# Masked words and conversion words in PSUM banks, casts of P on ScalarE alone, in a fused sparse-attention and feed-forward kernel

## The chip, the cores and the metric

The kernel runs on one core of one Trainium2 chip. A core has five engines, each with an instruction stream of its own that runs in order: TensorE (PE, matrix products; its weight loads are shown as PEld), VectorE (DVE), ScalarE (ACT), GpSimd (POOL) and SyncE (SP), which here only issues transfers. SBUF is the working memory of 128 partitions. PSUM is the memory that PE writes, in eight banks of 512 words a partition; DVE and ACT read and write it too, POOL doesn't. The metric is the device time of one execution in microseconds (us), the median of several runs.

## What is computed

Block-sparse attention over 4 × 8 heads of 768 positions with 64 dimensions, and behind it a feed-forward part in which g = h − tanh(h):

```python
scores = scale * np.matmul(q, k.transpose(0, 1, 3, 2))
...
scores = np.where(mask, scores, -1000000000.0)
scores = scores - np.max(scores, axis=-1, keepdims=True)
attn = np.exp(scores)
attn = attn / (np.sum(attn, axis=-1, keepdims=True) + 1e-09)
return np.matmul(attn, v).astype(np.float32)
...
h = x @ w_in
g = h - np.tanh(h)
return (g @ w_out).astype(np.float32)
```

`mask` lets a block of 32 positions see its neighbours, the first and the last block, and three drawn blocks. x is the attention's output, 3072 tokens of 512; w_in is 512 × 2048, w_out 2048 × 512. The inputs are 32-bit floats, but the weights arrive as 64-bit words that the kernel turns into 32-bit ones ("converts").

## The kernel before

**Precision by parts.** PE multiplies with fewer bits than the inputs have. So operands are split into a high and a low part, and products of parts are summed. For q and k, `mask_words` (line 183) clears the low 12 bits of each word (`bitwise_and` with −4096) and `low_words` (line 191) subtracts the result from the word: what is left is the low part `lo`, which lies in the same tile where the masked word lay. Each pair of heads has q and k side by side in one tile `rawx` of 1536 columns, handled as two halves of 768: both masks and the first subtraction run on DVE, the second subtraction on POOL. The tiles `lo` and `rawx` each have two buffers.

**The pieces of attention.** The heads go in 16 pairs (`pr`), and each pair has six steps `n` (96 in all). In a step PE makes three banks of trial scores for a row maximum (`smax`), which DVE reduces (`most`, tile `mc`), and three banks of final scores (`scores`), which ACT turns into exponentials (`exps`, tile `pe`). The exponentials P are split as well: `high` (line 292) casts them to 16 bits, tile `ph`, in two ACT operations of 768 columns, except for one step in six, `n % 6 in PH_DVE`, where DVE casts 1536 columns at once; `low` (line 301) takes the rest on POOL, tile `pl`. `accum` multiplies both with V (tile `vhl`), `norm` divides. The maxima of a head go back into the operands by a small transfer (`most_send`, tile `nm`). `pe` has three buffers, `ph` and `pl` four.

**Banks.** Two PSUM banks hold the products with V. The six others form a ring: whoever calls `bank()` gets the next one, and so must wait until the user of six calls before has been read out:

```python
        turn = iter(range(10**6))
        ps = lambda: banks[next(turn) % 6], banks[6:]
```

**The order.** Nothing is left to a scheduler here. `at(time, f, ...)` (line 342) collects pieces of work with due times; a step n has the length 2, a pair 12. The list is sorted by time (line 435) and carried out in that order, and each engine keeps to the order in which its instructions were written (class `InOrder`). SP's transfers go through one queue in the same order: the loads of `rawx`, the twelve transfers a pair that spread it and `lo` over the operand tiles `slot` (`dist`), `nm`, and the results.

**Conversions.** Six weight tiles are converted during attention: `load_pre` fetches 64-bit words, `convert_pre` (line 403) makes 32-bit ones by three DVE operations (`convert_op`, line 449), at due times 2 apart, and sends them out to memory. They recur every 24, so in every other pair. The feed-forward part converts the other tiles by the same three operations (`convert`, line 465), there with a PSUM bank for the words in between. That part (`FFN`) has an order of its own; the diff doesn't touch it.

Of the kernel before, what the change touches and what calls it, by code (L numbers as in the profile page):

```python
# [15 lines left out]
I32 = mybir.dt.int32  # L16
AF = mybir.ActivationFunctionType
ALU = mybir.AluOpType
# [24 lines left out]
W0, DW = 42.9, 24  # L43
# [7 lines left out]

LEAD = 12
LAV = 5.35
PH_DVE = (3,)
RAMP, NRAMP = 4, 24
LATE = {2: (14, 10, 6), 3: (8, 4, 3), 4: (5, 3, 2), 5: (2, 1, 1), 6: (1, 0.5, 0.5)}

# [32 lines left out]
@with_exitstack  # L90
def attention_ffn(ctx, tc, kq, v, samp, w_in, w_out, blocks, out):
    nc = tc.nc
    cst = ctx.enter_context(tc.tile_pool(name="cst", bufs=1))
    dpool = ctx.enter_context(tc.tile_pool(name="dpool", bufs=1, space=DRAM))
    xscr = [dpool.tile([P, T, DM], F32, name=f"xscr{b}") for b in range(B)]

    ident = cst.tile([P, P], F32, name="ident")
    make_identity(nc, ident)
    bias = [cst.tile([P, 1], F32, name=f"bias{i}") for i in range(2)]
    for x, val in zip(bias, (QB, THR2)):  # L100
        nc.vector.memset(x, val)

    slots = [cst.tile([P, 4, 2, S], F32R, name=f"slot{i}") for i in range(NSLOT)]
    wt = {(m, ft): dpool.tile([P, 512], F32, name=f"w{m}{ft}") for ft in range(NPRE) for m in "io"}
    part = [dpool.tile([P, DM], F32, name=f"part{j}") for j in range(CT)]
    f2 = ctx.enter_context(tc.tile_pool(name="f2", bufs=2))
    stage = [cst.tile([P, 1024], I32, name=f"stage{i}") for i in range(2)]
    ffn = FFN(tc, w_in, w_out, xscr, ident, bias, slots, wt, out, f2, part, stage)
    with ExitStack() as actx:
        psum = actx.enter_context(tc.tile_pool(name="psum", bufs=1, space=PSUM))  # L110
        banks = [psum.tile([P, 512], F32, name=f"ps{i}") for i in range(8)]
        turn = iter(range(10**6))
        ps = lambda: banks[next(turn) % 6], banks[6:]
        ffn.one = lambda name: ps[0]()
        ffn.nc = InOrder(tc)
        attention(actx, tc, kq, v, samp, w_in, w_out, blocks, xscr, ident, ps, slots, wt, f2, ffn)
        ffn.nc = tc.nc
    with ExitStack() as fctx:
        ffn.rest(fctx)


def attention(ctx, tc, kq, v, samp, w_in, w_out, blocks, xscr, ident, ps, slots, wt, f2, ffn):
    nc = InOrder(tc)
    bank, av = ps
# [5 lines left out]
    raws, rvs, los, ams, sbs = {}, {}, {}, {}, {}  # L130
# [49 lines left out]
    def half(pr, x):  # L180
        return slice(x * S, (x + 1) * S)

    def mask_words(pr, x):
        if x == 0:
            los[pr] = p2.tile([P, 2 * S], F32, tag="lo", name=f"lo{pr}", bufs=2)
        c = half(pr, x)
        nc.vector.tensor_scalar(
            out=los[pr].bitcast(I32)[:, c], in0=raws[pr].bitcast(I32)[:, c], scalar1=-4096, scalar2=None, op0=ALU.bitwise_and
        )

    def low_words(pr, x, eng):
        c = half(pr, x)
        eng.tensor_tensor(out=los[pr][:, c], in0=raws[pr][:, c], in1=los[pr][:, c], op=ALU.subtract)

    def dist(pr, j, what):
        i = pr % NSLOT
# [95 lines left out]
    def high(n, e):  # L292
        if e == 0:
            phs[n] = p2.tile([P, 2 * S], F16, tag="ph", name=f"ph{n}", bufs=PB)
        if n % 6 not in PH_DVE:
            c = half(None, e)
# [45 lines left out]
    def at(time, f, *args):  # L342
        ev.append((time, len(ev), f, args))
# [12 lines left out]
    for pr in range(NPAIR):  # L356
        t0 = 12 * pr
        late = LATE.get(pr, (0, 0, 0))
        at(t0 - 36 + late[0] if pr > 1 else -18.5 if pr else -49, load_x, pr)
        at(t0 - 15.5 if pr > 1 else 1 if pr else -18, load_v, pr)  # L360
        s = t0 + late[1]
        when = (s - 29.2, s - 25.2, s - 23.2) if pr > 1 else (-1, 0.7, 2.8) if pr else (-28, -28, -28)
        at(when[0], mask_words, pr, 0)
        at(when[1], mask_words, pr, 1)
        at(when[2], low_words, pr, 0, nc.vector)
        at(when[2], low_words, pr, 1, nc.gpsimd)
        for x, (j, what) in enumerate(ORDER):
            at(t0 + late[2] - 21 + x if pr > 1 else x - 3 if pr else EARLY[x], dist, pr, j, what)
        s = t0 + (10.5, 4)[pr] if pr < 2 else t0
        at(s - 9.3, v_most, pr)  # L370
        at(s - 7.54, v_turn, pr)
        at(s - 7.28, v_scale, pr)
        at(t0 + (8.45, 4, 0)[min(pr, 2)] - 4.45, v_parts, pr, 0)
        at(t0 + (7, 4, 0)[min(pr, 2)] - 2.3, v_parts, pr, 1)
        at(t0 + 16.4, spill, pr)
# [21 lines left out]
    wraw = {}  # L397
# [5 lines left out]
    def convert_pre(m, ft, k):  # L403
        if k == 0:
            wcv[m, ft] = f2.tile([P, 512], I32, tag="wcvt", name=f"cvt{m}{ft}")
        convert_op(nc, wraw[m, ft], wcv[m, ft], wcv[m, ft], k)
        if k == 2:
            nc.sync.dma_start(out=wt[m, ft], in_=wcv.pop((m, ft)).bitcast(F32))

    wcv = {}  # L410
    for x in range(2 * NPRE):
        at(W0 + DW * x, load_pre, "io"[x % 2], x // 2)
        for k in range(3):
            at(W0 + DW * x + 6 + 2 * k, convert_pre, "io"[x % 2], x // 2, k)
    xa = x_parts(slots[(NPAIR - 3) % NSLOT].rearrange("p a j s -> p (a j s)"))
    xn = {}

# [31 lines left out]
def convert_op(nc, raw, t, tmp, k):  # L449
    w = raw.rearrange("p (n w) -> p n w", w=2)  # L450
    if k == 0:
        nc.vector.tensor_scalar(
            out=tmp, in0=w[:, :, 1], scalar1=3, scalar2=0x3FFFFFF8, op0=ALU.logical_shift_left, op1=ALU.bitwise_and
        )
    elif k == 1:
        nc.vector.scalar_tensor_tensor(
            out=tmp, in0=w[:, :, 1], scalar=-0x40000000, in1=tmp, op0=ALU.bitwise_and, op1=ALU.bitwise_or
        )
    else:
        nc.vector.scalar_tensor_tensor(  # L460
            out=t, in0=w[:, :, 0], scalar=29, in1=tmp, op0=ALU.logical_shift_right, op1=ALU.bitwise_or
        )
# [18 lines left out]
def x_parts(area):  # L481
    n = NCT * P * CT
    return [area[:, i * n : (i + 1) * n].rearrange("p (c n) -> p c n", c=NCT) for i in range(2)]
# [224 lines left out]
```

## Time and profile before

| | us |
|---|---|
| three runs: median (lowest to highest) | 1006.49 (1005.1 to 1008.77) |
| the profiled execution | 1005.82 |
| its span, first to last instruction | 1004.0 |
| busy in the span: PE | 914.0 |
| DVE | 786.9 |
| ACT | 625.9 |
| POOL | 519.4 |

The busy times are of the whole span and mix its two halves, attention up to about 460 us and the feed-forward part behind it. In the rows below, an arrow reads "output from inputs" (`lo<-rawx` writes `lo` and reads `rawx`; a `pf` or `ps` is a PSUM bank), the shape is partitions × elements, `x3` counts merged instructions, and a bracket gives the idle time before an instruction and what ended it. L79 is the line of the helper through which all attention work is recorded, so there the tiles tell the operations apart.

### The profile page before, as it was taken

The numbers are of one execution on the slowest core, as the hardware profiler recorded it, in microseconds if no ns is written. First come the engines' busy times: TensorE is split into PE (matmuls) and PEld (weight loads), VectorE is DVE, ScalarE is ACT, GpSimd is POOL, SyncE is SP. The second block draws the span as 40 slices with busy tenths as digits, with TensorE's granted clock in tenths as the row PEclk, the third lists the DMA queues.
The fourth block names the chain that finished last, engine by engine and source line by source line (L and its number), as shares of the span: only waits on it lengthen the run. The fifth ranks groups of instructions, "written<-read, shape, count | busy, mean of one in ns | idle before, by whom it ended". The sixth has DMA issues, their size and how long they took to land.

```text
span 1004.0 us, 18122 instructions
## 1 busy us (share of the span) xinstructions
PE 914.0 (91%) x7072; PEld 752.5 (75%) x7072; DVE 786.9 (78%) x1222; ACT 625.9 (62%) x1013; POOL 519.4 (52%) x247
## 2 busy tenths in 40 slices
PE   2887889998988888977999999999999999999997
PEld 1676777776777776866778888888888888888885
DVE  5797999999999998837999976666676666667664
ACT  0576767777777776874666665554555565555553
POOL 2586987888788888792455532222222222222221
PEclk9898989899999999978999999999999999999999
DMA  8746676767676757334362210120020001001001
GB/s 218 190 113 150 166 194 162 179 169 179 169 179 163 187 138 164 112 105 138 113 191 79 85 64 22 37 79 22 1 74 1 1 1 43 1 0 43 1 1 42
DMA packets 54100, 99.74 MB, mean 99 GB/s; under 512 B 5768, under 2 KB 26440, under 8 KB 54016
## 3 DMA queue, kind: packets, MB, share of 16 engines
q1 hardware_dynamic: 53704, 97.81, 36.4%
q8 instruction: 55, 0.90, 0.4%
q10 hardware_dynamic: 312, 0.79, 0.3%
q14 instruction: 29, 0.24, 0.1%
HBM read 44.64 MB, written 15.20 MB: 60 GB/s over the span
## 4 chain that ended last, share of the span: by engine, by line
PE 62%; DVE 24%; DMA 7%; issue 4%; ACT 2%; SPq 0%; POOL 0%; DVEq 0%; ACTq 0%; POOLq 0%
PE pf L561 25%; PE ps L79 12%; DVE mc L79 9%; PE pf L593 8%; PE pf L594 8%; PE pf L595 8%; DVE lo L79 5%; DVE vhl L79 2%; DMA slot<-nm 2%; DMA slot<-lo 2%; DVE ph L79 1%; DMA xscr<-xq 1%; DVE xq L79 1%; PE pf L475 1%; DVE cvto L79 1%
## 5 line engine op out<-in xcount | busy, mean ns | idle before, releaser
L79 POOL TENSOR_TENSOR pl<-pe,ph 128x1536 f16<-128x1536 f32 x96 | 313.6, 3281 | 87.0 <-ACT ph L79 41.8
L79 PE MATMUL ps<-slot 89*128 89x512 f32 (+5 forms) x1152 | 271.1, 376 | 55.5 <-DVE mc L79 31.1
L584 POOL TENSOR_TENSOR gl<-t,gh 128x512 fp32r<-128x512 f32 x94 | 121.5, 1293 | 336.3 <-ACT gh L583 292.2
L79 PEld LDWEIGHTS ps<-slot 89*128 89x128 f32 (+2 forms) x1152 | 189.8, 205 | 89.8 <-DVE mc L79 44.6
L79 ACT ACTIVATE pe<-ps 128x512 f32<-128x512 f32 x288 | 169.1, 592 | 102.4 <-PE ps L79 94.2
L79 DVE TENSOR_REDUCE mc<-ps 128x1 f32<-128x512 f32 (+1 forms) x288 | 186.6, 679 | 25.8 <-PE ps L79 25.5
L576 DVE TENSOR_TENSOR t<-t,pf 128x512 f32<-128x512 f32 x94 | 64.5, 686 | 122.8 <-ACT t L570 122.7
L79 PEld LDWEIGHTS <-ph 128*128 128x128 f16 x2304 | 117.7, 101 | 27.5 <-issue 27.2
L79 ACT ACTIVATE ph<-pe 128x768 f16<-128x768 f32 x160 | 135.0, 844 | 5.0
L79 PE MATMUL ps<-vhl,ph 128*128 128x65 f16 (+1 forms) x2304 | 129.7, 200 | 3.2 <-DVE vhl L79 2.3
L583 ACT ACTIVATE gh<-t 128x512 fp32r<-128x512 f32 x94 | 59.4, 632 | 116.1 <-DVE t L580 114.1
L79 PE MATMUL ps<-vhl,pl 128*128 128x65 f16 x1152 | 124.4, 198 | 6.2 <-POOL pl L79 6.2
L79 PEld LDWEIGHTS <-pl 128*128 128x128 f16 x1152 | 111.8, 103 | 9.0 <-POOL pl L79 9.0
L568 ACT ACTIVATE u<-pf 128x512 f32<-128x512 f32 x94 | 56.2, 598 | 78.4 <-PE pf L561 78.0
L580 DVE COPY_PREDICATED t<-mk,pf 128x512 f32<-128x512 int32 x94 | 69.7, 742 | 6.9 <-DVE pf L579 0.5
L593 PE MATMUL pf<-wx,gh 128*128 128x512 f32 x192 | 74.7, 389 | 0.0
L594 PE MATMUL pf<-wx,gh 128*128 128x512 f32 x192 | 74.7, 389 | 0.0
L579 DVE SCALAR_TENSOR_TENSOR pf<-qq,pf 128x512 f32<-128x512 f32 x94 | 65.3, 694 | 7.5
L561 PE MATMUL pf<-slot,wx 128*128 128x512 f32 x288 | 70.3, 391 | 0.4 <-DVE t L580 0.4
L561 PE MATMUL pf<-xbuf,wx 128*128 128x512 f32 x288 | 69.5, 390 | 0.0
L572 ACT ACTIVATE qq<-u,bias 128x512 f32<-128x512 f32 x94 | 68.3, 727 | 0.0
L574 ACT ACTIVATE mk<-u,bias 128x512 f32<-128x512 f32 x94 | 67.8, 721 | 0.0
(113 smaller groups left out, 1564.2 us busy)
## 6 DMA issues: line engine op xcount, KB each, us to landing
slot<-rawx SPq DMA_DIRECT2D x128, 192.0 KB
slot<-lo SPq DMA_DIRECT2D x64, 192.0 KB
rawx<-kq SPq DMA_DIRECT2D x15, 768.0 KB
stage<-w_in SPq DMA_DIRECT2D x13, 512.0 KB
stage<-w_out SPq DMA_DIRECT2D x13, 512.0 KB
rawv<-v SPq DMA_DIRECT2D x16, 384.0 KB
xscr<-xq SPq DMA_DIRECT2D x16, 384.0 KB
out<-ob SPq DMA_DIRECT2D x24, 256.0 KB
```

Source lines behind the costliest of these rows:

```text
L79: r = f(*args, **kw)
L561: nc.tensor.matmul(h, lhsT=w[:, cc], rhs=x[:, c, :], start=(k == 0), stop=(k == 3 * NCT - 1))
L572: nc.scalar.activation(out=qq, in_=u, func=AF.Square, scale=QS, bias=qbias)
L574: nc.scalar.activation(out=mk, in_=u, func=AF.Relu, scale=-1.0, bias=tbias)
L576: nc.vector.tensor_tensor(out=t, in0=t, in1=h, op=ALU.subtract)
L579: nc.vector.scalar_tensor_tensor(out=h, in0=qq, scalar=QC, in1=h, op0=ALU.add, op1=ALU.mult)
L580: nc.vector.copy_predicated(t, mk.bitcast(I32), h)
L583: nc.scalar.activation(out=gh, in_=t, func=AF.Copy)
L584: nc.gpsimd.tensor_tensor(out=gl, in0=t, in1=gh.bitcast(F32), op=ALU.subtract)
L593: nc.tensor.matmul(o, lhsT=gh[:, c], rhs=wo[0][ft], start=(ft == f0), stop=False)
L594: nc.tensor.matmul(o, lhsT=gh[:, c], rhs=wo[1][ft], start=False, stop=False)
L595: nc.tensor.matmul(o, lhsT=gl[:, c], rhs=wo[0][ft], start=False, stop=(ft == f1 - 1))
```

## The change

- The masked words no longer lie in `lo`: each mask writes a bank of the ring, and the subtraction reads that bank and writes `lo`. The 1536 columns of a pair go in three pieces of 512 (a bank's size) in place of two halves. A piece's subtraction follows its mask at once, all on DVE; the three pieces are due at s − 29.2, s − 27.2 and s − 23.2. POOL's subtraction is gone.
- `PH_DVE` is empty: all casts to `ph` are ACT's, two in each step.
- In the six conversions of attention the words in between go to a bank of the ring; the three operations are due 0.45 apart in place of 2.

```diff
-PH_DVE = (3,)
+PH_DVE = ()
...
+    his = {}
+
     def mask_words(pr, x):
         if x == 0:
             los[pr] = p2.tile([P, 2 * S], F32, tag="lo", name=f"lo{pr}", bufs=2)
-        c = half(pr, x)
+        b = his[pr, x] = bank()
         nc.vector.tensor_scalar(
-            out=los[pr].bitcast(I32)[:, c], in0=raws[pr].bitcast(I32)[:, c], scalar1=-4096, scalar2=None, op0=ALU.bitwise_and
-        )
-
-    def low_words(pr, x, eng):
-        c = half(pr, x)
-        eng.tensor_tensor(out=los[pr][:, c], in0=raws[pr][:, c], in1=los[pr][:, c], op=ALU.subtract)
+            out=b.bitcast(I32), in0=raws[pr].bitcast(I32)[:, 512 * x : 512 * (x + 1)], scalar1=-4096, scalar2=None, op0=ALU.bitwise_and
+        )
+
+    def low_words(pr, x):
+        c = slice(512 * x, 512 * (x + 1))
+        nc.vector.tensor_tensor(out=los[pr][:, c], in0=raws[pr][:, c], in1=his.pop((pr, x)), op=ALU.subtract)
...
-        when = (s - 29.2, s - 25.2, s - 23.2) if pr > 1 else (-1, 0.7, 2.8) if pr else (-28, -28, -28)
-        at(when[0], mask_words, pr, 0)
-        at(when[1], mask_words, pr, 1)
-        at(when[2], low_words, pr, 0, nc.vector)
-        at(when[2], low_words, pr, 1, nc.gpsimd)
+        when = (s - 29.2, s - 27.2, s - 23.2) if pr > 1 else (-1, 0.7, 2.8) if pr else (-28, -28, -28)
+        for x in range(3):
+            at(when[x], mask_words, pr, x)
+            at(when[x], low_words, pr, x)
...
-        convert_op(nc, wraw[m, ft], wcv[m, ft], wcv[m, ft], k)
+            wcp[0] = bank().bitcast(I32)
+        convert_op(nc, wraw[m, ft], wcv[m, ft], wcp[0], k)
...
-            at(W0 + DW * x + 6 + 2 * k, convert_pre, "io"[x % 2], x // 2, k)
+            at(W0 + DW * x + 6.05 + 0.45 * k, convert_pre, "io"[x % 2], x // 2, k)
```

DVE's order around the first mask of pair 9 (`lo9` from `rawx9`; `ps` is a bank of the ring, `nm` the maxima sent), before:

```order
L79 TENSOR_SCALAR lo9_2882<-rawx9_2655 128x768
L79 TENSOR_REDUCE mc15_2878<-ps1_95 128x2
L79 TENSOR_REDUCE mc15_2878<-ps3_97 128x1
L79 CAST ph39_2888<-pe39_2872 128x1536
L79 TENSOR_REDUCE mc15_2878<-ps5_99 128x1
L79 TENSOR_SCALAR nm14_2949<-ps1_95 6x128
L79 TENSOR_REDUCE mc15_2878<-ps2_96 128x2
```

and now:

```order
L79 TENSOR_SCALAR ps1_95<-rawx9_2679 128x512
L79 TENSOR_TENSOR lo9_2906<-rawx9_2679,ps1_95 128x512
L79 TENSOR_REDUCE mc15_2902<-ps0_94 128x2
L79 TENSOR_REDUCE mc15_2902<-ps3_97 128x1
L79 TENSOR_REDUCE mc15_2902<-ps5_99 128x1
L79 TENSOR_SCALAR nm14_2975<-ps1_95 6x128
L79 TENSOR_SCALAR ps3_97<-rawx9_2679 128x512
L79 TENSOR_TENSOR lo9_2906<-rawx9_2679,ps3_97 128x512
L79 TENSOR_REDUCE mc15_2902<-ps2_96 128x2
```

The mask of 768 columns became mask and subtraction of 512, the cast is gone, and a second piece stands where only maxima stood. The third piece stands where the second mask and DVE's subtraction were, about one step apart.

ACT's order in step 63, the fourth of pair 10 (`pe63`), with the scaling of V (`vhl`) and the next step behind it, before:

```order
L79 ACTIVATE pe63_4538<-ps4_98 128x512
L79 ACTIVATE pe63_4538<-ps0_94 128x512
L79 ACTIVATE pe63_4538<-ps2_96 128x512
L79 ACTIVATE vhl2_110<-rawv11_4191,sb11_4477 128x12x64
L79 ACTIVATE pe64_4603<-ps4_98 128x512
```

and now:

```order
L79 ACTIVATE pe63_4574<-ps5_99 128x512
L79 ACTIVATE pe63_4574<-ps1_95 128x512
L79 ACTIVATE ph63_4591<-pe63_4574 128x768
L79 ACTIVATE pe63_4574<-ps4_98 128x512
L79 ACTIVATE vhl2_110<-rawv11_4226,sb11_4515 128x12x64
L79 ACTIVATE ph63_4591<-pe63_4574 128x768
L79 ACTIVATE pe64_4641<-ps0_94 128x512
```

The two casts of 768 columns came into this step, as they stand in the other five of the pair.

More of the change, by code (lines that the diff above doesn't have):

```diff
@@ L405, in convert_pre @@
             wcv[m, ft] = f2.tile([P, 512], I32, tag="wcvt", name=f"cvt{m}{ft}")
-        convert_op(nc, wraw[m, ft], wcv[m, ft], wcv[m, ft], k)
+            wcp[0] = bank().bitcast(I32)
+        convert_op(nc, wraw[m, ft], wcv[m, ft], wcp[0], k)
         if k == 2:
             nc.sync.dma_start(out=wt[m, ft], in_=wcv.pop((m, ft)).bitcast(F32))
-    wcv = {}
+    wcv, wcp = {}, [None]
     for x in range(2 * NPRE):
```

## The prediction

> **What bounds the kernel now.** I read the page's slices first, then the busy times by stage, then one period of VectorE (DVE) in order of time. The run has two halves. Attention ends near 460 us; then the feed-forward half runs with TensorE (PE) full.
>
> ```profile
> PE   2887889998988888977999999999999999999997
> DVE  5797999999999998837999976666676666667664
> PE 62%; DVE 24%; DMA 7%; issue 4%; ACT 2%; SPq 0%; POOL 0%; DVEq 0%; ACTq 0%; POOLq 0%
> ```
>
> The slices are 25.1 us each. In attention PE has eights and DVE nines; behind slice 20 PE has nines to the end. So what the change saves before 460 us moves the start of a PE-bound half by as much; nothing in the diff touches that half's own work.
>
> Attention treats one pair of heads after another, and each pair has one DVE CAST (of `ph`, n%6 = 3). The time between two CASTs is a period:
>
> ```profile
> 184.01:210.58 26.57, 24.30 (x293) 20.06 (x292) 26.29 (x41) 19.08 (x29) 22.32 (x7) 0.87 0.64 164
> 263.45:288.05 24.60, 21.78 (x293) 17.67 (x292) 24.15 (x38) 19.86 (x30) 22.04 (x7) 1.00 0.66 164
> 288.05:314.44 26.39, 23.53 (x293) 19.18 (x292) 26.11 (x42) 19.50 (x29) 22.28 (x7) 0.94 0.66 170
> 365.40:387.29 21.89, 19.60 (x273) 15.97 (x273) 21.38 (x38) 17.91 (x27) 20.87 (x7) 1.00 0.52 129
> ```
>
> The columns are length, busy PE, PE loads, DVE, ACT, POOL, then the granted clock. The plain period takes 24.60 us, and DVE is busy for 24.15 of it; no other engine passes 22.1. A period with three conversion operations (288.05) takes 1.79 more, and DVE's busy time grows by 1.96. A period with a mask fewer (365.40) takes 2.71 less, and DVE's falls by 2.77. The period follows DVE nearly one to one: **DVE is the bound of attention.**
>
> What DVE does there, in order of time (start, length):
>
> ```profile
> 263.45 0.94 DVE L79 CAST ph<-pe 128x1536 f16<-128x1536 f32 x1
> 264.32 0.68 DVE L79 TENSOR_REDUCE mc<-ps 128x1 f32<-128x512 f32 x1
> ...
> 269.82 1.99 DVE L79 TENSOR_SCALAR lo<-rawx 128x768 int32<-128x768 int32 x1
> 271.73 1.28 DVE L79 TENSOR_REDUCE mc<-ps 128x2 f32<-128x512 f32 x2
> ...
> 273.72 1.88 DVE L79 TENSOR_TENSOR lo<-rawx,lo 128x768 f32<-128x768 f32 x1
> 275.52 1.87 DVE L79 TENSOR_REDUCE mc<-ps 128x2 f32<-128x512 f32 x3
> ...
> 283.91 3.03 DVE L79 TENSOR_SCALAR lo<-rawx 128x768 int32<-128x768 int32 x1
> 286.85 1.28 DVE L79 TENSOR_REDUCE mc<-ps 128x2 f32<-128x512 f32 x2
> ```
>
> The same mask at the start of the run, with GpSimd (POOL) not yet at work, and the subtraction there:
>
> ```profile
> 8.03 0.95 DVE L79 TENSOR_TENSOR lo<-rawx,lo 128x768 f32<-128x768 f32 x1
> 18.73 0.55 DVE L79 TENSOR_SCALAR lo<-rawx 128x768 int32<-128x768 int32 x1
> ```
>
> So 0.55 us of mask becomes 1.99 and 3.03 beside POOL, whose `pl` operations last over 3 us each. Most of that time DVE stands and waits for POOL.
>
> **Part 1: masks into PSUM, low parts from there.** From start to next start the plain period loses 1.91 (269.82), 1.80 (273.72) and 2.94 (283.91): 6.65 us. It gains three pairs of a mask of 512 words into a bank and a subtraction that reads that bank. Attention shows no such operation; the feed-forward half shows its like: SBUF words into PSUM, then SBUF with PSUM.
>
> ```profile
> L452 DVE TENSOR_SCALAR pf<-stage x26: 678/691/720, 464.1 to 575.8; 128x512 int32<-128x512 int32 x26
> 464.06 0.69 DVE L452 TENSOR_SCALAR pf<-stage 128x512 int32<-128x512 int32 x1
> 464.79 0.69 DVE L456 SCALAR_TENSOR_TENSOR pf<-stage,pf 128x512 int32<-128x512 int32 x1
> 472.60 0.69 DVE L460 SCALAR_TENSOR_TENSOR cvti<-stage,pf 128x512 int32<-128x512 int32 x1
> 473.21 0.68 DVE L576 TENSOR_TENSOR t<-t,pf 128x512 f32<-128x512 f32 x1
> 500.00:550.00 50.00, 49.76 (x218) 40.55 (x218) 48.22 (x80) 32.92 (x58) 25.70 (x20) 1.00 0.45 137
> ```
>
> POOL is busy for half of that stretch (25.70 of 50.00), yet none of 26 took over 720 ns: the wait on POOL is gone in this form. A step with a dependent successor costs 0.73, one with an independent successor 0.61. A pair costs 1.34, three cost 4.0. Bounds: 0.55 and 0.95 (free, above) at the low end, 4.5 for three; today's waits stay at the high end, 3 × (1.91 + 1.80) = 11.1. I take 4.0, the row's. DVE: −2.65 per period.
>
> Left alone, the new form is the dearer one: 0.55 us for 768 words within SBUF against 0.69 for 512 into PSUM. Free operations would rise from 2 × 0.55 + 0.95 = 2.05 to 4.0, which is a rival below. The Trainium skill has this as a rule that speaks against the part ("VectorE: DVE Perf Modes", The perf-mode tier table: a 32-bit `tensor_scalar` within SBUF runs at twice the rate that it has with an operand in PSUM). The trace agrees as far as these two rows go, and by the rule alone the period would grow.
>
> The masks take banks from the ring of six. Some wait for the ACT read of what the bank held before (the mask into ps1 of pair 9 does). Behind it on DVE stand the maxima `mc`, for which PE waits. I take 0 to 0.6 us for each, inside the losses below.
>
> **Part 2: POOL** loses its `lo` operation, 2.54 us a period, and waits for a DVE cast:
>
> ```profile
> 264.48 10.30 POOL L79 TENSOR_TENSOR pl<-pe,ph 128x1536 f16<-128x1536 f32 x3 [2.56 <-DVE ph L79]
> 274.74 2.54 POOL L79 TENSOR_TENSOR lo<-rawx,lo 128x768 f32<-128x768 f32 x1
> 277.25 9.27 POOL L79 TENSOR_TENSOR pl<-pe,ph 128x1536 f16<-128x1536 f32 x3
> ```
>
> Its six `pl` are 19.6 us; it isn't the bound, so this is worth nothing by itself.
>
> **Part 3: the cast goes to ACT.** DVE loses 0.87 (263.45 to 264.32). ACT gets two:
>
> ```profile
> 266.31 1.25 ACT L79 ACTIVATE pe<-ps 128x512 f32<-128x512 f32 x2 [0.48 <-PE ps L79]
> 267.59 0.84 ACT L79 ACTIVATE ph<-pe 128x768 f16<-128x768 f32 x1
> 268.34 0.58 ACT L79 ACTIVATE pe<-ps 128x512 f32<-128x512 f32 x1
> 284.99 0.93 ACT L79 ACTIVATE vhl<-rawv,sb 128x768 f16<-128x768 f32 x1
> ```
>
> From start to start a cast is 0.75 and an exponential 0.64 (1.28 for two). ACT's period becomes 18 × 0.64 + 12 × 0.75 + 0.9 = 21.4.
>
> **What is late next.** DVE: 24.60 − 6.65 − 0.87 + 4.0 = 21.1. ACT: 21.4. POOL: 19.6. PE, from its best fed stretch:
>
> ```profile
> 264.39 0.24 PE L79 MATMUL ps<-vhl,ph 128*128 128x65 f16 x2
> 265.50 2.38 PE L79 MATMUL ps<-slot 128*128 128x512 f32 x12
> 267.72 0.24 PE L79 MATMUL ps<-vhl,ph 128*128 128x65 f16 x2
> ```
>
> 264.39 to 267.72 holds one n whole (36 products with V, 12 of scores and maxima): 3.33 us, six make 20.0 at full clock. So ACT and DVE end up level. Two engines that share six banks in order can't both run without gaps; today DVE alone loses 0.45 (24.60 − 24.15). I take 0.7 over ACT's sum, a choice: **22.1 a plain period, −2.5.** Floor 21.4, ceiling 24.6.
>
> **Part 4: the conversions.** Three SBUF operations come to PSUM too, and follow one another at 0.45 steps instead of 2:
>
> ```profile
> 300.12 2.04 DVE L79 TENSOR_SCALAR cvto<-rawo 128x512 int32<-128x512 int32 x1
> 304.94 0.75 DVE L79 SCALAR_TENSOR_TENSOR cvto<-rawo,cvto 128x512 int32<-128x512 int32 x1
> 308.86 0.68 DVE L79 SCALAR_TENSOR_TENSOR cvto<-rawo,cvto 128x512 int32<-128x512 int32 x1
> ```
>
> Now they cost the period 1.8; later 3 × 0.61 = 1.8 on DVE, which gives 22.9, and 23.5 with the losses: −2.9. Their SP transfer only comes earlier.
>
> **The sum.** Between the CASTs at 103.5 and 365.4 lie five plain periods and five with conversions: 5 × 2.5 + 5 × 2.9 = 27. Some run at a granted clock of 0.87 to 0.94 (rows above), where PE's 20.0 becomes over 21: −2. Before 103.5 two periods have waits for loads too: I give them 3 together. The period at 365.40 loses 4.6 of DVE work, gains 1.3, but has PE and ACT near 20: 1. After it there are no masks, and its end is ACT's:
>
> ```profile
> 443.64 0.84 ACT ph L79
> 444.48 0.49 ACT pe L79
> 445.00 0.85 ACT ph L79
> 445.88 0.56 POOL pl L79
> ```
>
> The last pair's two casts come into this chain: +1.5. In all 27 − 2 + 3 + 1 − 1.5 = 27.5. The profiled execution took 1005.82 us (span 1004.0, 1.8 around it), and the median of the three runs is 1006.49, so it is an ordinary one: 1005.8 − 27.5 = **978 us**.
>
> The rivals:
>
> - **ACT takes over as the bound with waits of its own.** At 21.4 it has the largest sum, and behind an exponential that waits for PE a cast waits too. If each of six n loses 0.35 us, the period is 23.5: −1.1 and −1.5, in all some 13 us: 992. For it: ACT idles 0.48 before `pe` even now. Against it: those gaps are PE waiting for DVE.
> - **Slower: mask banks stall DVE.** Three masks a period (and a conversion every other one) ask for a bank that ACT has yet to read. If ACT lags by an exponential and two casts (0.64 + 0.75 + 0.75 = 2.1) at each, DVE's period is 21.1 + 6.4 = 27.5, +2.9: ten make 29, about 1035. It turns from gain to loss at 1.2 us a mask. Against it: PE must have filled the banks between, so ACT is seldom over one operation behind.
> - **The waits stay.** POOL holds up the new form too: 11.1 instead of 4.0 makes 28.2 a period, +36 us in ten: 1042. Or the surplus over 0.55 isn't POOL's doing and passes to whatever comes next, and only the dearer form is left: −0.87 and 2.0 give +1.1 a period, 1017. The maximum of 720 ns in 26 speaks against the first, the regular 1.9 to 3.0 beside POOL against the second. (The second is what the skill's tier table would make of it.)
> - **More than I say.** No gaps at all: 21.4 plain and 22.9 with conversions save 5 × 3.2 + 5 × 3.5 = 33.5 in place of 27: 972. If PE's clock, which falls in periods with idle gaps, then stays up (the 2 come back) and the start gains 3 more: 967.
>
> **How the numbers follow.** Forecast 978 (970 to 986): 0.60. More than I say, below 970: 0.10. ACT bound, 986 to 1001: 0.17. Within 0.5% (1001 to 1011; about what a measurement of this kernel can tell from no change): 0.05. Slower: 0.05 by bank stalls, 0.02 by POOL's hold on the new form, 0.01 by its dearer price alone. Faster is 0.87, same 0.05, slower 0.08. The range 962 to 1000 leaves out the slower cases, no change and the edges of the rest.
>
> **What would show it.** Right: masks and subtractions of 512 at 0.6 to 0.75 us whatever POOL does; POOL's `pl` without idle before it for DVE; plain periods near 22 (they can be counted from one `vhl` of DVE to the next), ACT over 94% busy in them; the feed-forward half as long as before, 25 to 30 us earlier. Wrong: masks above 1 us or with idle before them for ACT (bank stalls); DVE near 90% and ACT idle for PE (a bound that I don't see, such as transfers of `nm`); a gain in the periods that is lost behind 440 us.

## The result, and the profile after

The changed kernel takes **963.93 us** (median of four runs, 962.25 to 966.77); the kernel before took 1005.8 beside it (four runs). The ratio is 0.9585, with an interval of 0.955 to 0.962. The profiled execution took 962.25 us, its span 960.2, so 43.8 us of span are gone. Of the ten executions with the masks alone (below) one took 1255.1 us at a granted clock of 0.66; it isn't in the ratio, and a later execution gave the profile.

The page after: PE's and DVE's slices, the granted clock, and the shares of the chain that ended last.

```profile
PE   2798899899989989779999999999999999999997
DVE  6798999899999977279999766766666675666664
PEclk9998999999999999889999999999999999999999
PE 73%; DVE 11%; DMA 7%; ACT 4%; issue 3%; POOL 1%; SPq 0%; DVEq 0%; ACTq 0%; POOLq 0%
```

DVE's share of the chain fell from 24% to 11%, PE's rose from 62% to 73%. PE has taken over as the bound, also in attention. The windows show it; each goes from one start of `vhl` on DVE (the low part of v, once a pair) to the next. The columns are length, busy PE, PE loads, DVE, ACT, POOL, then the granted clock, DMA share and GB/s.

```profile
172.18:196.69 24.51, 21.52 (x293) 17.62 (x293) 21.75 (x43) 20.71 (x32) 19.25 (x7) 1.00 0.78 187
196.69:217.75 21.06, 20.65 (x293) 17.67 (x293) 19.98 (x41) 20.39 (x32) 19.30 (x7) 1.00 0.81 201
217.75:240.34 22.59, 21.21 (x293) 17.62 (x293) 21.68 (x43) 20.59 (x32) 19.31 (x7) 1.00 0.78 202
329.15:349.24 20.09, 20.09 (x282) 17.12 (x282) 17.75 (x37) 19.46 (x30) 18.32 (x7) 1.00 0.66 155
```

The plain period (196.69) went from 24.60 to 21.06, and PE is busy for 20.65 of it. ACT has 20.39 and DVE 19.98: three engines lie within 0.7 us of each other. A period with conversions takes 22.59, or 24.51 where PE also waits for a transfer of `nm`.

The operations themselves, first the masks grouped by form (busy time, mean ns of one, idle time before them), then masks, subtractions and `vhl` with the shortest, median and longest ns:

```profile
L79 DVE TENSOR_SCALAR ps<-rawx 128x512 int32<-128x512 int32 x48 | 32.7, 681 | 0.0
```
```profile
L79 DVE TENSOR_SCALAR ps<-rawx x48: 671/682/694, 7.8 to 334.0; 128x512 int32<-128x512 int32 x48
L79 DVE TENSOR_TENSOR lo<-rawx,ps x48: 686/686/691, 8.5 to 334.7; 128x512 f32<-128x512 f32 x48
```
```profile
L79 DVE SCALAR_TENSOR_TENSOR vhl<-rawv,sb,vhl x16: 1007/1416/3409, 38.6 to 375.5; 128x768 f16<-128x768 f32 x16
```

All 48 masks and all 48 subtractions took 671 to 694 ns, whatever POOL was doing. No mask waited for a bank (idle 0.0). Where the 43.8 us lie is read from the starts of `vhl`, before:

```profile
108.63 1.87 DVE L79 SCALAR_TENSOR_TENSOR vhl<-rawv,sb,vhl 128x768 f16<-128x768 f32 x1
368.26 2.10 DVE L79 SCALAR_TENSOR_TENSOR vhl<-rawv,sb,vhl 128x768 f16<-128x768 f32 x1
391.20 2.11 DVE L79 SCALAR_TENSOR_TENSOR vhl<-rawv,sb,vhl 128x768 f16<-128x768 f32 x1
418.64 2.11 DVE L79 SCALAR_TENSOR_TENSOR vhl<-rawv,sb,vhl 128x768 f16<-128x768 f32 x1
```

and after:

```profile
102.37 2.56 DVE L79 SCALAR_TENSOR_TENSOR vhl<-rawv,sb,vhl 128x768 f16<-128x768 f32 x1
329.15 1.41 DVE L79 SCALAR_TENSOR_TENSOR vhl<-rawv,sb,vhl 128x768 f16<-128x768 f32 x1
349.24 2.40 DVE L79 SCALAR_TENSOR_TENSOR vhl<-rawv,sb,vhl 128x768 f16<-128x768 f32 x1
375.49 2.38 DVE L79 SCALAR_TENSOR_TENSOR vhl<-rawv,sb,vhl 128x768 f16<-128x768 f32 x1
```

The first row of each is the fourth pair's, the second the fourteenth's. Up to the fourth 6.3 us were gained; in the **ten periods** between (259.6 before, 226.8 after) 32.9; in the next period 2.9, in the one after 1.2; and from there to the end 0.7 (585.4 against 584.7). These ten periods serve as the measure below.

One row didn't fit my forecast: `vhl` itself. The change doesn't touch it, yet in the ten periods it fell from 2.1 to mostly 1.4 us. It is the one long DVE operation of a period that still reads two inputs from SBUF. The experiments led back to it.

### The profile page after: what moved, and what is told of

The parts are those of the page before. It is cut to its first block, busy times and chain, and to the rows that moved or that the text cites. A ratio compares the mean times of both kernels' runs of the same rounds, so it can differ in the third digit from the quotient of the medians.

```text
span 960.2 us, 18142 instructions
## 1 busy us (share of the span) xinstructions
PE 891.2 (93%) x7072; PEld 740.1 (77%) x7072; DVE 736.6 (77%) x1254; ACT 642.7 (67%) x1045; POOL 474.8 (49%) x231
## 4 chain that ended last, share of the span: by engine, by line
PE 73%; DVE 11%; DMA 7%; ACT 4%; issue 3%; POOL 1%; SPq 0%; DVEq 0%; ACTq 0%; POOLq 0%
PE pf L563 25%; PE ps L79 24%; PE pf L595 8%; PE pf L596 8%; PE pf L597 8%; DMA slot<-nm 3%; DVE mc L79 3%; ACT pe L79 2%; DVE ps L79 2%; DMA slot<-lo 1%; PE pf L477 1%; DVE vhl L79 1%; POOL pl L79 1%; DMA slot<-rawx 1%; DVE pf L579 1%
## 5 line engine op out<-in xcount | busy, mean ns | idle before, releaser
L79 POOL TENSOR_TENSOR pl<-pe,ph 128x1536 f16<-128x1536 f32 x96 | 308.0, 3214 | 90.6 <-ACT ph L79 67.2
L79 PE MATMUL ps<-slot 89*128 89x512 f32 (+5 forms) x1152 | 254.0, 365 | 43.4 <-DMA slot<-nm 14.3
L79 PEld LDWEIGHTS ps<-slot 89*128 89x128 f32 (+2 forms) x1152 | 182.3, 199 | 72.1 <-DMA slot<-nm 18.2
L79 ACT ACTIVATE pe<-ps 128x512 f32<-128x512 f32 x288 | 166.1, 588 | 42.0 <-PE ps L79 37.8
L79 ACT ACTIVATE ph<-pe 128x768 f16<-128x768 f32 x192 | 161.8, 843 | 5.6
L79 PEld LDWEIGHTS <-ph 128*128 128x128 f16 x2304 | 112.9, 99 | 25.8 <-issue 25.3
L79 PE MATMUL ps<-vhl,ph 128*128 128x65 f16 (+1 forms) x2304 | 124.7, 197 | 2.5 <-DVE vhl L79 1.9
L79 PE MATMUL ps<-vhl,pl 128*128 128x65 f16 x1152 | 119.6, 195 | 5.5 <-POOL pl L79 5.5
L79 PEld LDWEIGHTS <-pl 128*128 128x128 f16 x1152 | 109.0, 101 | 7.9 <-POOL pl L79 7.9
```

What stands on the lines that cost most here:

```text
L79: r = f(*args, **kw)
```

## The experiments

### The three parts, one at a time

First, is it the place of the words or only the new order? The changed kernel with the masked words in SBUF, all else as changed:

```diff
-        b = his[pr, x] = bank()
+        b = his[pr, x] = los[pr][:, 512 * x : 512 * (x + 1)]
```

> The changed kernel, but each mask of 512 words writes its place in lo (SBUF) and the subtraction works there in place; pieces, order, engines, casts and conversions stay. Theory W (DVE's waits for POOL were the loss, and words in PSUM end them): masks and subtractions take 1.2 to 3 us beside POOL again in place of 0.69, DVE's plain period grows from 21.1 to 25 or more, and the time is 1000 or more, no better than before the change (1006). Rival O (what helped is the order: small pieces early, nothing left on POOL): operations stay near 0.7 and the time within 964 to 970.

Measured: 1019.22 us, ratio 1.0142 (1.0119 to 1.0164): slower than before the change. In a view of the operations that read `rawx` (min, median, max ns):

```profile
L79 DVE TENSOR_SCALAR lo<-rawx x48: 412/1556/3315, 7.6 to 391.7; 128x512 int32<-128x512 int32 x48
L79 DVE TENSOR_TENSOR lo<-rawx,lo x48: 691/693/3519, 8.0 to 392.2; 128x512 f32<-128x512 f32 x48
```

Free, a mask within SBUF is quicker than one into a bank, 412 ns against 671. Beside POOL it takes 1556 at the median. So the dearer form is the cheaper one here, and the bank is what the gain needs: 55 us lie between the two placements. Theory W held, though from 182 us on its plain periods took 24.0 to 25.9, not all of them the 25 or more that I had put down.

Then the masks' part alone, on the kernel before:

```diff
-        c = half(pr, x)
+        b = his[pr, x] = bank()
...
+        for x in range(3):
+            at(when[x], mask_words, pr, x)
+            at(when[x], low_words, pr, x)
```

> The kernel before with the masked words in PSUM and the subtractions on DVE alone; DVE still casts one step in six and converts within SBUF. Theory W: most of the gain is here; masks near 0.69 us, POOL without lo, plain period 21.5 to 22.3, time 970 to 978. Rival C (the cast's move is what freed the period, since POOL waited 2.6 us a period for it): 990 or more.

the casts' part alone:

```diff
-PH_DVE = (3,)
+PH_DVE = ()
```

> The kernel before with all casts on ACT and nothing else. Theory W: DVE loses 0.87 us a period and keeps its waits for POOL, so 23.7 a plain period at best, 993 to 1002; the masks may wait longer, since POOL no longer pauses for the cast. Rival C: 980 or less.

and the conversions' part alone:

```diff
-        convert_op(nc, wraw[m, ft], wcv[m, ft], wcv[m, ft], k)
+            wcp[0] = bank().bitcast(I32)
+        convert_op(nc, wraw[m, ft], wcv[m, ft], wcp[0], k)
...
-            at(W0 + DW * x + 6 + 2 * k, convert_pre, "io"[x % 2], x // 2, k)
+            at(W0 + DW * x + 6.05 + 0.45 * k, convert_pre, "io"[x % 2], x // 2, k)
```

> The kernel before with the six conversions' words in PSUM banks and closer together, nothing else. Theory W: the first operation of each falls from 2.0 to 0.7 us, but the next mask then waits for POOL longer, so a period with conversions gains 0 to 1.4 us: 999 to 1006. Rival: the dearer PSUM form and the banks cost, 1006 to 1010.

Measured: masks alone 998.93 (ratio 0.9933, 0.9908 to 0.9958), casts alone 988.93 (0.9848, 0.9825 to 0.9872), conversions alone 1009.68 (1.0042, 1.0011 to 1.0074). All three missed what I had put down. Masks alone won 7 us where I expected 28 to 36, casts alone more than expected, conversions alone lost a little. Rival C's number held for the masks but not for the casts (980 or less), and the rival's number held for the conversions. The three single effects add up to some 20 us; together they give 42.

### One part taken back

The changed kernel with the old conversions (the reverse of the last diff):

> The changed kernel with the six conversions within SBUF and 2 apart as before; masks in PSUM and casts on ACT stay. Theory S (masks and casts each leave the other's limit in place, and only both together let PE become the bound; conversions are a side matter): 966 to 973, plain periods still 21.1, those with conversions 1 to 1.5 us longer. Rival V (the conversions' words within SBUF still hold DVE and undo much of the gain): 978 or more.

Measured: 985.37 us, ratio 0.9815 (0.9771 to 0.9859): three operations in every other period are worth 21 us. The rival's number held. Two plain periods of that run, with one between them that has a conversion:

```profile
155.89:176.31 20.42, 20.00 (x291) 17.04 (x290) 19.53 (x40) 19.77 (x31) 18.99 (x7) 1.00 0.85 204
199.90:224.61 24.71, 21.88 (x290) 18.37 (x289) 22.49 (x41) 19.78 (x31) 18.48 (x6) 0.93 0.69 171
```

Neither has a conversion in it. The first is as short as any, the second takes 4.3 us more. At its head stand these, from DVE's and POOL's timelines:

```profile
199.90 3.93 DVE L79 SCALAR_TENSOR_TENSOR vhl<-rawv,sb,vhl 128x768 f16<-128x768 f32 x1
199.89 3.12 POOL L79 TENSOR_TENSOR pl<-pe,ph 128x1536 f16<-128x1536 f32 x1 [0.29 <-PE ps L79]
```

`vhl` came 0.01 us after a `pl` of POOL, and ended 0.82 after it had ended (203.83 against 203.01).

The changed kernel with the sixth cast back on DVE:

```diff
-PH_DVE = ()
+PH_DVE = (3,)
```

> The changed kernel with the cast of one step in six back on DVE; masks and conversions stay in PSUM. Theory S: the DVE cast waits in order for ACT's exponentials and POOL waits for the cast, so the period stays near 23.5: 985 to 1000. Rival (casts alone gave 17 us only because they relieved DVE; with masks in PSUM DVE has room for 0.9 us): 964 to 970.

Measured: 995.17 us, ratio 0.9897 (0.9874 to 0.992), inside theory S's range, but not by its mechanism: DVE had no idle time before any cast but the first. The cast's own 0.9 us a period can't make up 31 us either. DVE and POOL at the head of a plain period, that period's window, and the longest waits in it (us in total, times, longest):

```profile
206.06 3.87 DVE L79 SCALAR_TENSOR_TENSOR vhl<-rawv,sb,vhl 128x768 f16<-128x768 f32 x1
206.00 3.11 POOL L79 TENSOR_TENSOR pl<-pe,ph 128x1536 f16<-128x1536 f32 x1
206.06:231.10 25.04, 22.41 (x294) 18.68 (x293) 23.21 (x42) 19.29 (x30) 19.10 (x7) 0.93 0.72 176
ACT pe L79 <- PE ps L79: 5.3, 5, 3.2
PEld ps L79 <- DVE mc L79: 3.5, 2, 2.9
POOL pl L79 <- ACT ph L79: 3.3, 2, 3.0
```

Again `vhl` starts just behind a `pl`, and waits it out. Behind it on DVE stand the maxima `mc`; PE waits for them, ACT waits for PE, and POOL for ACT. The masks' part alone has the same fault: a second look at that kernel gave 999.99 us and showed `vhl` at 3060 ns on average over its 16, most at 3.87.

> The kernel before with masks in PSUM alone, once more, for a profile at the full clock. Theory S: masks at 0.69 us and no wait for POOL in them, yet a plain period of 24 or so: DVE idle before its cast for ACT's exponentials, or maxima waiting for PE, and POOL idle before pl for DVE's cast by 2 us or more a period. Rival: the masks wait for their banks, with idle time in front of them for ACT.

```profile
L79 DVE SCALAR_TENSOR_TENSOR vhl<-rawv,sb,vhl x16: 997/3868/3894, 37.9 to 414.7; 128x768 f16<-128x768 f32 x16
```

In the ten periods the plain ones took 23.66 to 25.35 us and the masks to 0.67 to 0.70, as theory S has it. But its reasons fell in part, and so did the rival: no cast but the first and no mask had idle time before it (POOL did idle before its `pl` behind the cast, mostly 1.1 to 2.5 us).

The same pairing in the kernel before and in the changed one, where the two starts lie otherwise. Before (POOL's `pl`, then DVE):

```profile
264.48 3.12 POOL L79 TENSOR_TENSOR pl<-pe,ph 128x1536 f16<-128x1536 f32 x1 [2.56 <-DVE ph L79]
266.31 2.10 DVE L79 SCALAR_TENSOR_TENSOR vhl<-rawv,sb,vhl 128x768 f16<-128x768 f32 x1
```

and after:

```profile
194.16 3.12 POOL L79 TENSOR_TENSOR pl<-pe,ph 128x1536 f16<-128x1536 f32 x1 [1.13 <-PE ps L79]
196.69 1.41 DVE L79 SCALAR_TENSOR_TENSOR vhl<-rawv,sb,vhl 128x768 f16<-128x768 f32 x1
197.37 3.72 POOL L79 TENSOR_TENSOR pl<-pe,ph 128x1536 f16<-128x1536 f32 x1
```

267.60 + 0.81 = 268.41, and 197.28 + 0.82 = 198.10: in these four kernels, and in the six others of this document that keep this form of it, `vhl` ends 0.81 to 0.82 us after the `pl` in progress, without exception. How long it seems to take is only a matter of when in that `pl` it came: 2.53 us behind its start costs 1.41, 1.83 behind costs 2.10, 0.01 behind costs 3.93. And the next `pl` is late in its turn (3.72 in the last row in place of 3.12).

### The low part of v taken out of it

That gave theory T: what each part alone lacked was that `vhl` was left to land at the head of a `pl`. To test it I took the kernel of 995.17, cast on DVE, and had ACT copy the high part of v into two banks, so that `vhl` reads one input from SBUF and one from PSUM:

```diff
-            nc.vector.scalar_tensor_tensor(
-                out=vv[:, :, 65:129], in0=vf, scalar=sbs[pr], in1=vv[:, :, 0:64], op0=ALU.mult, op1=ALU.subtract
-            )
+            for x in (0, 6):
+                h = bank()[:, 0:384].rearrange("p (n d) -> p n d", d=D)
+                nc.scalar.activation(out=h, in_=vv[:, x : x + 6, 0:64], func=AF.Copy)
+                nc.vector.scalar_tensor_tensor(
+                    out=vv[:, x : x + 6, 65:129], in0=vf[:, x : x + 6], scalar=sbs[pr], in1=h, op0=ALU.mult, op1=ALU.subtract
+                )
```

> This is the changed kernel with the sixth cast back on DVE (the run that took 995.2 us, plain period 25.1 us, the low part of v 3.88 us in it), and in addition the low part of v reads its high part from two PSUM banks, into which ACT copies it (2 copies of 384 columns, some 0.5 us each by the 0.58 of an exp of 512), in two DVE operations of 384 columns. Theory T (the cost of the cast was that the low part of v, the one DVE operation left with two inputs in SBUF, lands where it waits out a whole GpSimd subtraction): the two pieces take 0.5 to 0.7 us each whatever GpSimd does, DVE's sum in a plain period falls from 23.7 to about 21, PE's 20.65 sets the period again: plain periods 21.1 to 21.8, 964 to 978 us. Rival U (the cast on DVE itself ties DVE, GpSimd and ACT together; the long low part only takes room that DVE would have had to wait in anyway): the pieces are short too, but DVE waits instead, plain periods stay at 24 or above, 985 us or more.

Measured: **970.62 us**, ratio 0.9659 (0.9632 to 0.9686), 25 us less, with the cast still on DVE. The two pieces of `vhl`, and two periods, plain and with conversions:

```profile
L79 DVE SCALAR_TENSOR_TENSOR vhl<-rawv,sb,ps x32: 605/608/616, 39.0 to 380.2; 128x384 f16<-128x384 f32 x32
197.35:218.82 21.47, 20.84 (x294) 17.68 (x293) 20.46 (x42) 19.96 (x32) 18.68 (x7) 1.00 0.82 199
218.82:241.78 22.96, 21.43 (x294) 17.61 (x293) 22.16 (x45) 20.14 (x32) 18.70 (x7) 1.00 0.78 196
```

608 ns at the median and 616 at most: no piece waited for POOL. The plain period fell from 25.04 to 21.47 and is PE's again. The ten periods fell by 26.5 us (255.1 to 228.6), and `vhl` itself lost 24.5: nine of its ten had taken 3.87, the first 1.00, and now each takes 1.13. So the cast, with ACT's two copies, costs only 0.4 us a plain period against the changed kernel, and rival U fell.

The combination not yet run, casts and conversions without the masks (the two diffs above, on the kernel before):

> This is the kernel before with two parts of the change, the casts all on ScalarE and the conversions' words in PSUM, and the masks and q/k low parts as before (in SBUF, one low part of two on GpSimd). It is the combination not yet run: casts alone 988.9, conversions alone 1009.7, masks and casts 985.4, masks and conversions 995.2, all three 963.9. If what counts is that no long DVE operation with two inputs in SBUF is left beside GpSimd (theory T), the masks' and low parts' operations keep the slow kind of period here: plain periods 22.8 to 24, 978 to 992 us. Rival: casts and conversions together make the step and the masks only add their own 2.65 us a period over sixteen periods less what PE's floor takes: plain periods 21.5 to 22.3, 966 to 976 us.

Measured: 984.54 us, ratio 0.9787 (0.9764 to 0.981), as T has it. Masks and subtractions within SBUF are left there, and wait:

```profile
L79 DVE TENSOR_SCALAR lo<-rawx x32: 548/1996/3085, 7.7 to 352.6; 128x768 int32<-128x768 int32 x32
```

Then the masks' part alone with `vhl` from PSUM, and `vhl` from PSUM alone on the kernel before:

> This is the kernel before with the masks' part of the change alone (998.9 us so far, the low part of v 3.06 us on average) and the low part of v from PSUM as in the run before this one. The sixth cast is on DVE and the conversions work in SBUF as before. Theory T (the masks' part missed its worth because the low part of v then waited out a whole GpSimd subtraction): the low part of v falls to two of 0.61 us, plain periods come to 21.3 to 22.3 us, and the conversions in SBUF cost some 0.5 to 1.5 us in each of eight periods more than in the run of 970.6: 972 to 984 us. Rival (the conversions in SBUF, or the cast, hold the slow kind of period by themselves): 988 us or more.

> This is the kernel before with one change that the change under study does not have: the low part of v reads its high part from PSUM. Masks, low parts of q and k, the cast on DVE and the conversions are as before. If only the low part of v mattered, its 2.1 us would become 1.2 and the periods fall as far as with the masks too: 972 to 984 us. If, as theory T has it, every DVE operation that works within SBUF beside GpSimd can land where it waits (masks 1.4 to 1.7 us here, low part of q and k 1.9, cast 1.1 to 1.2), the wait moves to the next of them and no more than 0.9 us in each of sixteen periods is won: 990 to 1006 us.

Measured: 977.79 us (ratio 0.9722, 0.9688 to 0.9756) and 993.22 (0.9869, 0.9843 to 0.9895), both inside T's ranges. The masks' part, worth 7 us by itself, is worth 15 once `vhl` no longer waits (993.2 to 977.8). And `vhl` alone brings 13, not the 22 to 34 of a kernel in which only it mattered, because other operations within SBUF then wait longer: the cast went from 1253 ns on average to 1386, the masks from 1742 to 1779.

| parts on the kernel before | us | ten periods | `vhl`, mean of 16, us |
|---|---|---|---|
| none | 1005.8 | 259.6 | 2.06 |
| masks | 998.9 | 257.6 | 3.06 |
| casts | 988.9 | 241.9 | 1.75 |
| conversions | 1009.7 | 263.9 | 2.05 |
| masks, casts | 985.4 | 241.2 | 2.32 |
| masks, conversions | 995.2 | 255.1 | 3.08 |
| casts, conversions | 984.5 | 243.3 | 1.78 |
| all three (the change) | 963.9 | 226.8 | 1.76 |
| `vhl` from PSUM alone | 993.2 | 252.4 | 2 × 0.60 |
| masks, `vhl` from PSUM | 977.8 | 237.0 | 2 × 0.61 |
| masks, conversions, `vhl` from PSUM | 970.6 | 228.6 | 2 × 0.61 |

### A version that beats both

In the changed kernel PE is the bound and still stands 14.3 us in all for transfers of `nm`, part of it late in attention:

```profile
PE ps L79 <- DMA slot<-nm: 3.8, 1, 3.8
349.24:375.49 26.25, 22.41 (x298) 18.86 (x295) 19.44 (x37) 20.42 (x32) 19.26 (x7) 0.93 0.61 141
```

So I let the transpose and the sending of the maxima come one unit of time earlier:

```diff
-        late = 0 if h < 4 else 2
+        late = 0 if h < 4 else 1
```

> The changed kernel with the maxima turned and sent one time unit (half a step) earlier from head 4 on. If the PE waits of 1.7 to 3.8 us for the transfer of nm (four in all, 14.3 us with the first) are on the path, each shrinks by up to 1.8: 958 to 962. Rival: PE then waits for DVE's joined maxima instead, 964 or more.

Measured: **957.15 us**, ratio 0.9521 (0.9503 to 0.9538), the best of all and just below the range that I had put down. The same period now:

```profile
345.96:367.38 21.42, 20.59 (x298) 17.50 (x295) 19.44 (x37) 20.14 (x32) 19.22 (x7) 1.00 0.64 158
```

It lost 4.8 of its 26.25 us, and PE's wait for `nm` over the whole run went from 14.3 to 8.2, all of it in the first 60 us.

## Why the prediction was right, and where its size was off

The forecast was 978 (962 to 1000); it came to 963.9, close to the lower end. That is below both figures of the rival "more than I say" (972 and 967), to which I gave a chance of 0.10. Direction and mechanism held; the sum was 16 us short of the span's 43.8. Point by point:

- **DVE was the bound, and the masks' waits were POOL's.** Right. In PSUM form all of them take 0.67 to 0.69, and a pair 1.32 from start to start (I had 1.34). With the words in SBUF the time is 1019.
- **The rule of the tier table** (the Trainium skill, "VectorE: DVE Perf Modes", The perf-mode tier table) gives the right order for a free engine: 412 ns against 671, though 1.6 times as long and not twice. It doesn't decide here: the rival that rested on it (1017) fell.
- **Bank stalls** did not come: no mask idled for ACT.
- **DVE's sum** was to be 21.1 with 0.45 of gaps, so 20.65 busy. It is 19.98. The missing 0.67 is `vhl`, which I left at its old 2.10 and which measured 1.41.
- **ACT's sum** was to be 21.4 and set the period. It is 20.39. I counted an exponential at 0.64 from start to start, taken where ACT had just waited for PE; in the plain period after, a single one mostly has 0.61 and two together 1.10 to 1.29, and all eighteen make 10.9 where I counted 11.5. The floor that I built on was 1.0 above the busy time; short gaps, which busy time leaves out, are the other part.
- **PE's floor** was to be 20.0; it is 20.65, and it is the bound that I named only third.
- **The chosen loss of 0.7** was for engines that block one another over banks. PE's period is 0.41 longer than its busy time (21.06 − 20.65). ACT's 21.4 + 0.7 = 22.1 was thus the **step that was mis-sized**: 21.06 to 21.13 in four of the five plain periods (the first, at 102.37, still took 24.50, with DVE busy for 23.34). Plain periods gave 15.5 where I had 12.5, those with conversions 17.4 where I had 14.5.
- **−2 for PE's clock** hardly came: the granted clock is 1.00 in nine of the ten periods and 0.93 in one. In the ten periods this makes 32.9 in place of 25.
- **Outside them**: start 6.3 (I had 3), the next period 2.9 (1), the rest 1.9 (−1.5, a cost). The casts on ACT cost the end of attention nothing that can be seen.

What the prediction lacked altogether, though its total doesn't show it, is that the parts don't add. My working gave each part its own share of DVE's time: 2.65 for the masks, 0.87 for the cast, the rest for the conversions. Alone, the masks brought 7 us, and the conversions cost 4. The shares assume that the waits which stay do not change. They do: the wait of `vhl` can be anything from nothing to a whole `pl`, and each part alone moved it or left others that wait. That the change got 1.4 rather than 3.9 there is a matter of where `vhl` happened to fall, and for the forecast it was luck. With the old conversions it fell at the head of a `pl` in four pairs; the four periods behind are 14 us longer than in the changed kernel, of the 21 us that are gone. Where `vhl` can't wait, the same conversions cost 7 (977.8 against 970.6; with all casts on ACT this wasn't run).

Why `vhl` starts at the head of a `pl` again and again can be read where the cast is on DVE. Here are the cast, the next two `pl` and `vhl`, first in the run of 995.17, then in the one of 970.62:

```profile
201.89 0.95 DVE L79 CAST ph<-pe 128x1536 f16<-128x1536 f32 x1
202.92 6.20 POOL L79 TENSOR_TENSOR pl<-pe,ph 128x1536 f16<-128x1536 f32 x2 [1.16 <-PE ps L79]
193.17 0.95 DVE L79 CAST ph<-pe 128x1536 f16<-128x1536 f32 x1
194.20 6.19 POOL L79 TENSOR_TENSOR pl<-pe,ph 128x1536 f16<-128x1536 f32 x2 [1.16 <-PE ps L79]
197.35 1.13 DVE L79 SCALAR_TENSOR_TENSOR vhl<-rawv,sb,ps 128x384 f16<-128x384 f32 x2
```

In every kernel with casts on DVE, POOL starts a `pl` 0.08 us after each such cast ends (the bracket names PE here, but the distance to the cast is the same throughout). In these two runs the second `pl` then starts 4.1 us after the cast began, and DVE reaches `vhl` without a pause after 4.17, just behind it. In the kernel before it was 2.86 (263.45 to 266.31); the 1.31 more are the mask and the subtraction that the new order puts in between. Where `vhl` doesn't wait (970.62, 977.79) the 4.17 is still there. So the order of the work puts the two starts together, and not the wait. One thing stays open: with the old conversions and all casts on ACT `vhl` starts 0.01 to 0.02 us behind a `pl` in four pairs, and no run shows why.

## What to carry to other kernels

Before removing one of several waits of one kind, list every operation that can wait for the same thing, and ask where each of them will land; a removed wait may turn up at the next. The price of such an operation is not a duration but a range, from free to free plus the whole operation of the other engine, and the parts of a change are worth their sum only when none is left. If one is left on the path, take it out as well, even by a dearer form, rather than trust its phase. (Three kernels with the cast on DVE gained 13 to 25 us by it; on the changed kernel itself it wasn't run.)

## What the runs showed of the hardware

- DVE's `vhl`, two inputs in SBUF, and POOL's `pl` excluded each other for whole operations: DVE ended 0.81 to 0.82 us after the `pl` in ten kernels, and the next `pl` was held in turn (3.72 in place of 3.12). The Trainium skill ("SBUF — State Buffer", Who interferes with whom) states such an exclusion for a DVE instruction with two SBUF inputs beside a GpSimd one that reads SBUF, and none for one with at most one SBUF input, as long as it doesn't run in a mode that uses both of its ports. The traces agree: 605 to 616 ns with the second input in PSUM.
- I had not expected the sharpness: an operation of 1.0 us takes 3.93 when it comes 0.01 us behind the other's start, and 1.41 when it comes 2.53 behind. With the masks alone, one that came 0.09 us ahead of a `pl` took 1.00, and that `pl` 3.89.
- Two inputs in SBUF are not the only case: in the kernel before, masks (one input) took 546 to 3078 ns and the cast 944 to 2712, while the maximum of v, also one input of 768 columns in SBUF, took 935 to 944 in all 16 pairs, 13 of them started inside a `pl`. Why it is spared no run isolates.

```profile
L79 DVE CAST ph<-pe x16: 944/946/2712, 46.6 to 439.5; 128x1536 f16<-128x1536 f32 x16
L79 DVE TENSOR_REDUCE am<-rawv x16: 935/938/944, 28.6 to 406.2; 128x1 f32<-128x768 f32 x16
```

- The profile counts such a wait as busy time of the operation that waits: the `vhl` of 3.93 us has no idle time before it and names no releaser. Only the comparison with its shortest durations shows it.
- The granted clock was 1.00 in three of the ten periods before (0.87 to 0.94 in the others) and in nine of the ten after. What sets it the windows don't show: before, a period in which PE idled 2.82 of 24.60 us had 1.00 and one in which it idled 2.27 of 26.57 had 0.87.
